# Input norms ahead of the segments, one column-tiled stretch per attention unit, feature-map adds on VectorE

## The chip, the core and the metric

One core of a Trainium2 chip runs the kernel. The metric is the device time of one execution in microseconds (us). TensorE is called PE in the rows, its weight loads PEld; DVE is VectorE, ACT is ScalarE, POOL is GpSimd, SP is SyncE, whose queue issues every DMA.

## What is computed

The input x has 2048 tokens of 1024 values (bf16). Cut to what matters, the reference is:

```python
n = layernorm(x)
q, k, v = n @ wq, n @ wk, n @ wv          # 32 heads of 32
M, z = 0, 0
for s in range(4):                        # segments of 512 tokens
    p = softmax(qs @ ks.T * scale + causal_mask)
    a_dot = p @ vs
    a_mem = (phi(qs) @ M) / (phi(qs) @ z + 1e-6)
    o = g * a_mem + (1 - g) * a_dot       # g = sigmoid(beta), per head
    M, z = M + phi(ks).T @ vs, z + phi(ks).sum()
h = x + concat(o) @ wo
out = h + (silu(m @ w1) * (m @ w3)) @ w2  # m = layernorm(h), inner width 3584
```

phi(t) is t + 1 where t > 0 and exp(t) elsewhere.

## The kernel before, in words

**Order.** The program first records all operations in a graph (`Graph`, L58), with what each reads, writes and costs, and a class: lower classes go first. `Graph.schedule` (L181) then plays the graph forward with those costs and fixes one order for each engine; `Graph.emit` (L311) writes it out with semaphore waits. So on the chip each engine runs its list in order, and an instruction that waits holds up all behind it on its engine. This is so for SP too: a load whose buffer isn't free yet holds up the loads behind it.

**Stages.** `run` (L934) records: constants, the norm and the projections of segment 0, then for each segment s: the norm of segment s+1 (`ln1`, L640), its projections (`qkv`, L653), the memory update (`memory`, L689), the attention (`attention`, L733) and the output projection with residual and second norm (`wo_stage`, L855). After that come two blocks of the feed-forward part of 1024 tokens each (`ffn_up` L878, `ffn_down` L910).

**Input norm.** `ln1` loads four tiles of 128 tokens into `xs`, of which there are two buffers (L460). `ln` (L622) takes statistics on DVE (L628, L630), the power -0.5 on POOL (L634, L636) and normalises on DVE (L637). PE transposes (L549), ACT or DVE copies the result (L560, L561) into `xnT`, of which there is one (L461): it is free again only when the projections of the segment before are done.

**Projections.** Weights come in six loads of 1 MB into three buffers `wp`; PE makes groups of eight matmuls of 512 columns (L537). Groups of full-size matmuls share two PSUM banks, 6 and 7 (`dense_group`, L523).

**Attention.** A unit (L743) is four heads of a segment; there are 32. It makes scores in three batches in PSUM banks 0 to 3 with four 32-row matmuls side by side (L763), exponentials on ACT (L778: eA, eB, eC), causal masks on POOL (L783), and then the sums with v and with ones in banks 4 and 5, four 32-column matmuls side by side (L814). These last are eight separate operations of PE, which the plan places one by one:

```python
for gr, what in ((gn, "n"), (gd, "d")):
    for kc, src in pieces():
        ...
        o = G.op("pe", 60 + (512 - 128 * kc) / 2.4, emit, reads=reads, cls=1, group=gr)
        o.mode = "col"
```

DVE inverts the sums (L824 to L844); from segment 1 on, the memory part is multiplied and added on POOL (L850, L852).

**Feature map.** `phi` (L677) makes exp on ACT, a min and a max on DVE (L682, L684) and their sum on POOL (L686), for keys (`pk`) and queries (`pq`), 24 times.

Of the kernel before, what the change touches and what calls it, by code (L numbers as in the profile page):

```python
# [10 lines left out]
BF16 = DT.bfloat16  # L11
# [5 lines left out]
class Op:  # L17
# [4 lines left out]
                 "mode", "bytes", "kind", "snap", "gate")  # L22

    def __init__(self, engs, cost, emit, cls, seq):
        self.engs, self.cost, self.emit, self.cls, self.seq = engs, cost, emit, cls, seq
        self.eng = None
        self.deps, self.users = {}, []
        self.missing = 0
        self.ready = 0.0
        self.start = self.end = None  # L30
        self.pos = None
        self.signal = False
        self.tok = None
        self.group = None
# [5 lines left out]
        self.gate = None  # L40

# [15 lines left out]

class Graph:  # L58
# [5 lines left out]
    SWITCH = 60.0  # L64
# [25 lines left out]
    def region(self, ap):  # L90
        where = self.base.get(ap.tensor.name)
# [3 lines left out]
        size = SIZE[ap.dtype]  # L95
        if space == "sb":
# [4 lines left out]
            dims = list(ap.ap)  # L101
            np_ = dims[0][1]
            ext = sum((n - 1) * abs(s) for s, n in dims[1:])
            return space, p0, p0 + np_, off + f0 * size, off + (f0 + ext + 1) * size
        ext = sum((n - 1) * abs(s) for s, n in ap.ap)
        return space, 0, 1, ap.offset * size, (ap.offset + ext + 1) * size

    def _touch(self, op, ap, write):
# [3 lines left out]
        space, p0, p1, lo, hi = reg  # L112
        step = self.PAGE if space == "sb" else 1 << 18
        for page in range(lo // step, (hi - 1) // step + 1):
            recs = self.pages.setdefault((space, page), [])
            keep = []
            for r in recs:
                o, w, a, b, c, d = r
                over = a < p1 and p0 < b and c < hi and lo < d
                if over and o is not op and (write or w):  # L120
                    self.dep(op, o, raw=w and not write)
                    if write and p0 <= a and b <= p1 and lo <= max(c, page * step) \
                            and min(d, (page + 1) * step) <= hi:
                        continue
                keep.append(r)
            keep.append((op, write, p0, p1, lo, hi))
            self.pages[(space, page)] = keep
# [7 lines left out]
    def op(self, engs, cost, emit, reads=(), writes=(), cls=5, deps=(), group=None,  # L135
           opens=False, closes=False, kind=None, gate=None):
# [6 lines left out]
        o.gate = gate  # L143
        if gate is not None:
# [7 lines left out]
        if group is not None:  # L152
            o.group = group
# [27 lines left out]
    def schedule(self):  # L181
# [15 lines left out]
        def offer(o):  # L197
            for e in o.engs:
                heapq.heappush(avail[e], (o.cls, o.seq, o))

        for o in ops:
            if o.missing == 0:
                offer(o)
        now = 0.0
        started = set()

        def can_start(o):
            g = o.group
            if g is None or g.banks is not None:
                return True  # L210
# [16 lines left out]
        while n_done < len(ops):  # L227
            moved = True
            while moved:
                moved = False  # L230
                for e in ENGINES:
# [4 lines left out]
                    while avail[e]:  # L236
                        item = heapq.heappop(avail[e])
                        o = item[2]
                        if o in started:
                            continue  # L240
                        if not can_start(o):
# [19 lines left out]
                    o.end = now + cost  # L261
# [21 lines left out]
            if what == "free":  # L283
                free[x] = True
            elif what == "pe":
# [5 lines left out]
            else:  # L291
# [8 lines left out]
                if g is not None:  # L300
# [96 lines left out]
def pool_ns(n):  # L397
    return 220.0 + n * 1.05
# [6 lines left out]
class Kernel:  # L405
# [13 lines left out]
    def plan(self):  # L419
# [40 lines left out]
        self.xs = [buf(f"xs{i}", [128, 1024], BF16) for i in range(2)]  # L460
        self.xnT = buf("xnT", [128, 8, 512], BF16)  # L461
# [30 lines left out]
        for i, off in enumerate((r1 + 16384, r2 + 4096)):  # L492
# [73 lines left out]
    def pool_op(self, f, n, reads, writes, cls=4):  # L566
        return self.g.op("pool", pool_ns(n), lambda e, gr: [f(e)], reads=reads, writes=writes,
                         cls=cls)
# [52 lines left out]

    def ln(self, k, src, dst, cls):  # L622
# [3 lines left out]
        for c in range(2):  # L626
            a, b = self.lnst[:, k, 6 * c:6 * c + 6], src[:, c * 512:(c + 1) * 512]
            self.dve_op(lambda e, a=a, b=b: e.bn_stats(a, b), dve_ns(512), [b], [a], cls)  # L628
        st2 = self.lnst[:, k, :].rearrange("p (a b) -> p a b", a=2)
        self.dve_op(lambda e: e.bn_aggr(mv, st2), 200.0, [st2], [mv], cls)  # L630
# [5 lines left out]
        self.pool_op(lambda e: e.tensor_tensor(rs, ve, mh, op=ALU.pow), 300, [ve, mh], [rs], 0)  # L636
        self.dve_op(lambda e: e.tensor_scalar(dst, src, mean, rs, op0=ALU.subtract,  # L637
                                              op1=ALU.mult), 540.0, [src, mean, rs], [dst], cls)

    def ln1(self, s):  # L640
        for i in range(4):
            t = 4 * s + i
            x = self.xs[t % 2][:, :]
            self.g.dma(x, self.x2d[t * 128:(t + 1) * 128, :], cls=0 if s == 0 else 2)
            self.ln(t, x, x, 2)
            gr = self.dense_group()
            self.transposes(gr, [(c * 128, self.xs[t % 2][:, c * 128:(c + 1) * 128])
                                 for c in range(8)], 2)
            out = self.xnT[:, :, i * 128:(i + 1) * 128]
# [3 lines left out]
    def qkv(self, s):  # L653
        p = s % 2
        for half in range(2):
            for kind in "qkv":
# [3 lines left out]
                self.g.dma(w[:, :, :], self.w[kind][:, half * 512:(half + 1) * 512].rearrange(  # L660
                    "(c p) n -> p c n", p=128), cls=1)
                for i in range(4):
                    gr = self.dense_group()
                    if kind == "v":
                        items = [(lambda gr: self.bank(gr), self.xnT[:, c, i * 128:(i + 1) * 128],
# [3 lines left out]
                    else:  # L669
                        items = [(lambda gr: self.bank(gr), w[:, c, i * 128:(i + 1) * 128],  # L670
                                  self.xnT[:, c, :], c == 0, c == 7, 512) for c in range(8)]
# [3 lines left out]
                    self.evac(gr, out, 512, view, cls=3)  # L675

    def phi(self, src, dst, cls):  # L677
# [5 lines left out]
                    [e_], [e_], cls)  # L683
        self.dve_op(lambda e: e.tensor_scalar(r, src, 0.0, None, op0=ALU.max), dve_ns(1024, 4),  # L684
                    [src], [r], cls)
        self.pool_op(lambda e: e.tensor_tensor(dst, e_, r, op=ALU.add), 1024, [e_, r], [dst],  # L686
                     cls)

    def memory(self, s):  # L689
# [3 lines left out]
        for pr in range(4):  # L693
# [29 lines left out]
            self.pool_op(lambda e, Mb=Mb, am=am, bl=bl: e.tensor_tensor(Mb, am, bl, op=ALU.mult),  # L723
                         256, [am, self.blk[:, :]], [Mb], 4)
# [18 lines left out]
    def unit(self, s, g, q, k, v, pq):  # L743
# [61 lines left out]
        for gr, what in ((gn, "n"), (gd, "d")):  # L805
            for kc, src in pieces():
                def emit(e, gr, kc=kc, src=src, what=what):
                    ins = []
                    b = gr.banks[0]
# [8 lines left out]
                    return ins  # L818

                reads = [src, v[:, kc, g, 0:128] if what == "n" else self.ones32[:, :]]  # L820
                o = G.op("pe", 60 + (512 - 128 * kc) / 2.4, emit, reads=reads, cls=1, group=gr)
                o.mode = "col"
# [4 lines left out]
        if s:  # L827
            td = t1v[:, :, 1:2]
            self.dve_op(lambda e: e.tensor_scalar(td, td, 1e-6, None, op0=ALU.add), 160.0,
                        [td], [td], 0)  # L830
# [16 lines left out]
        if s:  # L847
            spread(R1, 1)
            Nm = self.Nm[:, :]
            self.pool_op(lambda e: e.tensor_tensor(o2, Nm, R1, op=ALU.mult), 512, [Nm, R1],  # L850
                         [o2], 2)
            self.pool_op(lambda e: e.tensor_tensor(oT, o1, o2, op=ALU.add), 512, [o1, o2],  # L852
                         [oT], 2)

    def wo_stage(self, s):  # L855
        oT = self.oT[s % 2]
        for i in range(4):
# [3 lines left out]
            for half in range(2):  # L861
                gr = self.dense_group()
                self.mms(gr, [(lambda gr: self.bank(gr), oT[:, c, i * 128:(i + 1) * 128],
                               self.wo[:, c, half * 512:(half + 1) * 512], c == 0, c == 7, 512)
                              for c in range(8)], 5)
# [7 lines left out]
            gr = self.dense_group()  # L873
# [4 lines left out]
    def ffn_up(self, blk):  # L878
        for ch in range(14):
            n = self.n_w13  # L880
            self.n_w13 += 1
# [129 lines left out]
```

## Time and profile before

| | us |
|---|---|
| median of 3 runs (1021.6 to 1023.35) | 1021.63 |
| the profiled execution, its own time | 1023.85 |
| its span, first to last instruction | 1022.1 |
| PE matmul busy | 947.3 (93%) |
| DVE busy | 418.9 (41%) |
| ACT busy | 320.6 (31%) |
| POOL busy | 235.2 (23%) |
| read from HBM / written | 76.55 MB / 8.39 MB |

The rows are of one execution. Matmuls overlap each other, so a busy PE isn't PE at its peak; the granted clock says at what share of its full speed PE was let run. A busy share over the whole span mixes stages that have different limits, so the stretches are read one by one.

### The profile page before, as it was taken

The numbers are of one execution on the slowest core, as the hardware profiler recorded it, in microseconds if no ns is written. First come the engines' busy times: TensorE is split into PE (matmuls) and PEld (weight loads), VectorE is DVE, ScalarE is ACT, GpSimd is POOL, SyncE is SP. The second block draws the span as 40 slices with busy tenths as digits, with TensorE's granted clock in tenths as the row PEclk, the third lists the DMA queues.
The fourth block names the chain that finished last, engine by engine and source line by source line (L and its number), as shares of the span: only waits on it lengthen the run. The fifth ranks groups of instructions, "written<-read, shape, count | busy, mean of one in ns | idle before, by whom it ended". The sixth has DMA issues, their size and how long they took to land.

```text
span 1022.1 us, 13535 instructions
## 1 busy us (share of the span) xinstructions
PE 947.3 (93%) x5639; PEld 419.5 (41%) x5744; DVE 418.9 (41%) x710; ACT 320.6 (31%) x353; POOL 235.2 (23%) x317
## 2 busy tenths in 40 slices
PE   0899899689968999999999999999999999999998
PEld 0334344234433333344444444444444444444443
DVE  2355662766457474546343343111133333332111
ACT  1367454777266766512111111000011111110000
POOL 2244333787178765400000000000000000000000
PEclk9999899899997999999999999999999999999999
DMA  7223233212330230486222332111123222210110
GB/s 257 77 71 132 94 103 124 73 52 84 124 105 1 83 104 22 114 294 186 73 58 78 83 83 83 33 30 42 42 83 88 83 63 83 62 57 26 42 42 26
DMA packets 101965, 85.82 MB, mean 84 GB/s; under 512 B 3088, under 2 KB 89104, under 8 KB 101904
## 3 DMA queue, kind: packets, MB, share of 16 engines
q1 hardware_dynamic: 101904, 84.95, 26.9%
q8 instruction: 45, 0.74, 0.3%
q14 instruction: 16, 0.13, 0.0%
HBM read 76.55 MB, written 8.39 MB: 83 GB/s over the span
## 4 chain that ended last, share of the span: by engine, by line
PE 78%; POOL 7%; DVE 7%; ACT 2%; DMA 2%; issue 2%; SPq 1%; DVEq 0%; ACTq 0%; POOLq 0%
PE ps L537 72%; PE ps L814 3%; POOL pk L686 2%; POOL pq L686 2%; PE ps L763 2%; DMA xs<-in_A_x_dram 1%; SPq L176 1%; PE ps L549 1%; DVE h L868 1%; POOL oT L852 1%; POOL eC L783 1%; DVE phe L682 1%; POOL o L850 1%; DVE phr L684 1%; ACT phe L512 1%
## 5 line engine op out<-in xcount | busy, mean ns | idle before, releaser
L537 PE MATMUL ps<-hnT,w1b 128*128 128x512 bf16 x879 | 221.9, 379 | 2.4 <-DMA w1b<-in_B_w_dram 1.4
L537 PE MATMUL ps<-hnT,w3b 128*128 128x512 bf16 x875 | 221.2, 379 | 1.1
L898 ACT ACTIVATE sg<-ps 128x512 bf16<-128x512 f32 x112 | 66.9, 597 | 420.7 <-PE ps L537 420.7
L537 PE MATMUL ps<-w2b,hm 128*128 128x512 bf16 x877 | 195.2, 379 | 1.0
L901 DVE SCALAR_TENSOR_TENSOR t<-sg,ps 128x512 bf16<-128x512 bf16 x112 | 76.9, 687 | 224.2 <-ACT sg L898 224.2
L537 PEld LDWEIGHTS ps<-w2b,hm 128*128 128x128 bf16 x896 | 87.7, 98 | 105.7
L537 PEld LDWEIGHTS ps<-hnT,w1b 128*128 128x128 bf16 x896 | 87.2, 98 | 106.1 <-issue 5.1
L537 PEld LDWEIGHTS ps<-hnT,w3b 128*128 128x128 bf16 x896 | 87.1, 98 | 104.9 <-issue 0.9
L537 PE MATMUL ps<-xnT,wp 128*128 128x512 bf16 x492 | 122.3, 390 | 6.1 <-ACT xnT L560 3.4
L906 DVE SCALAR_TENSOR_TENSOR hm<-t,ps 128x512 bf16<-128x512 bf16 x112 | 76.8, 686 | 34.9 <-PE ps L537 31.8
L928 DVE TENSOR_TENSOR ob<-hr,ps 128x512 bf16<-128x512 bf16 x32 | 22.0, 687 | 143.4 <-PE ps L537 143.4
L537 PEld LDWEIGHTS ps<-xnT,wp 128*128 128x128 bf16 x512 | 46.7, 100 | 63.1 <-issue 15.4
L537 PE MATMUL ps<-wp,xnT 128*128 128x512 bf16 x244 | 61.3, 380 | 2.7 <-DVE v L561 1.4
L778 ACT ACTIVATE eA<-ps 128x2048 bf16<-128x2048 f32 x32 | 60.0, 1874 | 10.7 <-PE ps L763 9.0
L537 PE MATMUL ps<-wo,oT 128*128 128x512 bf16 x248 | 59.8, 379 | 1.2 <-DVE h L868 0.5
L778 ACT ACTIVATE eB<-ps 128x1536 bf16<-128x1536 f32 x32 | 46.4, 1449 | 18.0 <-PE ps L763 18.0
L778 ACT ACTIVATE eC<-ps 128x1536 bf16<-128x1536 f32 x32 | 46.3, 1448 | 17.1 <-PE ps L763 16.2
L783 POOL TENSOR_SCALAR_AFFINE_SELECT eC<-eC 128x512 bf16<-128x512 bf16 x64 | 41.9, 655 | 21.6 <-ACT eC L778 20.5
L549 PE MATMUL ps<-ident,xs 128*128 128x128 bf16 x128 | 13.2, 265 | 28.3 <-DVE xs L637 26.0
L763 PE MATMUL ps<-qT,kT 32*128 32x256 bf16 (+3 forms) x512 | 36.1, 315 | 2.8 <-ACT eC L778 1.4
L824 DVE STREAM_TRANSPOSE T<-ps 128x512 f32<-128x512 f32 x32 | 22.8, 712 | 31.9 <-PE ps L814 31.9
L537 PEld LDWEIGHTS ps<-wo,oT 128*128 128x128 bf16 x256 | 23.4, 98 | 29.5 <-issue 3.8
(88 smaller groups left out, 765.9 us busy)
## 6 DMA issues: line engine op xcount, KB each, us to landing
w1b<-in_B_w_dram SPq DMA_DIRECT2D x28, 512.0 KB, 3.9
w3b<-in_B_w_dram SPq DMA_DIRECT2D x28, 512.0 KB, 4.7
wp<-in_A_wq_dram SPq DMA_DIRECT2D x8, 1024.0 KB, 4.9
wp<-in_A_wk_dram SPq DMA_DIRECT2D x8, 1024.0 KB, 4.9
wp<-in_A_wv_dram SPq DMA_DIRECT2D x8, 1024.0 KB, 5.1
w2b<-in_B_w_dram SPq DMA_DIRECT2D x7, 1024.0 KB, 8.8
xs<-in_A_x_dram SPq DMA_DIRECT2D x16, 256.0 KB, 2.8
xr<-in_A_x_dram SPq DMA_DIRECT2D x16, 256.0 KB, 2.9
```

Of the source, the lines that this page charges most:

```text
L537: return [e.matmul(p[0](gr), p[1], p[2], start=p[3], stop=p[4]) for p in part]
L549: return [e.transpose(b[:, c:c + 128], s, self.ident[:, :]) for c, s in items]
L686: self.pool_op(lambda e: e.tensor_tensor(dst, e_, r, op=ALU.add), 1024, [e_, r], [dst], cls)
L763: ins.append(e.matmul(self.bank(gr, j, n, off), k[r, g, 128 * kc:128 * kc + 128], q[r, g, 128 * kc:512], start=True, stop=True, tile_posit ...
L778: return [e.activation(et[:, :, :], src, AF.Exp, scale=self.scale)]
L783: self.pool_op(lambda e, m=m: e.affine_select(m, m, pattern=[[0, 4], [1, 128]], compare_op=ALU.is_ge, fill=0.0, base=0, channel_multiplier ...
L814: ins.append(e.matmul(self.ps[r, b * 512 + 128 * kc:(b + 1) * 512], lhsT, src[:, j, :], start=first, stop=True, tile_position=(0, 32 * j), ...
L824: G.op("dve", dve_ns(512), lambda e, gr: [e.transpose(T1, self.bank(gr))], writes=[T1], cls=0, group=gd)
L898: self.g.op("act", act_ns(512), lambda e, gr, sg=sg: [e.activation(sg, self.bank(gr), AF.Tanh, scale=0.5)], writes=[sg], cls=2, group=gg)
L901: e.scalar_tensor_tensor(t1, sg, 1.0, self.bank(gr), op0=ALU.add, op1=ALU.mult)], reads=[sg], writes=[t1], cls=2,
L906: e.scalar_tensor_tensor(dst, t1, 0.5, self.bank(gr), op0=ALU.mult, op1=ALU.mult)], reads=[t1], writes=[dst], cls=2,
L928: self.g.op("dve", dve_ns(512), lambda e, gr, hs=hs, ob=ob: [e.tensor_tensor(ob, hs, self.bank(gr), op=ALU.add)], reads=[hs], writes=[ob], ...
```

## The change

1. `ln1` of segments 1 to 3 is recorded ahead of the segments. Their transposed results go to buffers that are otherwise used later: segments 1 and 2 to those of the first two hidden norms (`hnT`), segment 3 to the one that segment 0 has left. `xs` has four buffers in place of two. While segment 0 is normed, banks 4 and 5 serve beside 6 and 7.
2. One tile of the first segment takes its statistics on ACT. The first 1 MB of weights comes in two loads of 256 columns. Sixteen matmuls on zeros run on PE at the start.
3. The eight column-tiled operations of a unit become one, which claims banks 4 and 5 together and reads all three exponentials. The planner lets it wait up to 2.6 us for a moment at which PE is not among full-size matmuls.
4. The sum in `phi` is on DVE; its max is on DVE or ACT. The product with the block mask and the multiply and add of the memory part are on POOL or DVE, whichever is free first in the plan.
5. The output projections of segments 2 and 3 are recorded among the first feed-forward block, after chunks 3 and 7 of 14, in a later class.
6. Costs that the planner uses are other numbers (among them the change of PE's tiling, 105 in place of 60 ns, and POOL's), it counts a port that DVE and POOL share, copies out of the projections have class 1 in place of 3, and overlaps of strided regions are found exactly.

The diff, cut to its core:

```diff
-    SWITCH = 60.0
+    SWITCH = 105.0
...
-def pool_ns(n):
-    return 220.0 + n * 1.05
+def pool_ns(n, inputs=1):
+    return 170.0 + n * (0.88 if inputs == 1 else 2.1)
...
-        self.xs = [buf(f"xs{i}", [128, 1024], BF16) for i in range(2)]
-        self.xnT = buf("xnT", [128, 8, 512], BF16)
+        self.xs = [buf(f"xs{i}", [128, 1024], BF16) for i in range(4)]
+        xn = buf("xnT", [128, 8, 512], BF16)
+        self.xnT = [xn, hnT01[0], hnT01[1], xn]
...
+                        if o.patience and mode == "full" and now < o.offered + o.patience:
+                            skipped.append(item)
...
+        w = self.oT[1][:, 0, :]
+        self.dve_op(lambda e: e.memset(w, 0.0), 300.0, [], [w], 0)
+        gr = self.dense_group()
+        wl = self.oT[1][:, 0, 0:128]
+        self.mms(gr, [(lambda gr: self.bank(gr), wl, w, True, True, 512)] * 16, 0, split=16)
...
+    def either(self, f, n, inputs, reads, writes, cls, mode=1, first="pool"):
+        engs = ("pool", "dve") if first == "pool" else ("dve", "pool")
+        return self.g.op(engs, {"pool": pool_ns(n, inputs), "dve": dve_ns(n, mode)},
+                         lambda e, gr: [f(e)], reads=reads, writes=writes, cls=cls, port=True)
...
+    def ln_act(self, k, src, dst):
+        sm, nm, sq = (self.lnst[:, k, i:i + 1] for i in range(3))
+        junk = self.oT[0][:, 0:2, :].rearrange("p a b -> p (a b)")
+        G = self.g
+        G.op("act", act_ns(1024), lambda e, gr: [e.activation(junk, src, AF.Copy, accum_out=sm)],
+             reads=[src], writes=[junk, sm], cls=1)
+        self.act(nm, sm, AF.Copy, 190.0, cls=1, scale=-1.0 / 1024)
+        G.op("act", act_ns(1024, 1), lambda e, gr: [e.activation(
+            junk, src, AF.Square, bias=nm, accum_out=sq)], reads=[src, nm], writes=[junk, sq],
+            cls=1)
...
     def ln1(self, s):
...
-            x = self.xs[t % 2][:, :]
+            x = self.xs[t % 4][:, :]
...
-            self.ln(t, x, x, 2)
-            gr = self.dense_group()
+            if t == 1:
+                self.ln_act(t, x, x)
+            else:
+                self.ln(t, x, x, 2 if s == 0 else 5)
+            gr = self.dense_group() if s else Group([(6,), (7,), (4,), (5,)], safe=True)
...
-            out = self.xnT[:, :, i * 128:(i + 1) * 128]
+            out = self.xnT[s][:, :, i * 128:(i + 1) * 128]
...
+                if n == 0:
+                    self.g.dma(w[:, :, 0:256], src[:, :, 0:256], cls=1)
+                    self.g.dma(w[:, :, 256:512], src[:, :, 256:512], cls=1)
+                else:
+                    self.g.dma(w[:, :, :], src, cls=1)
...
-        self.pool_op(lambda e: e.tensor_tensor(dst, e_, r, op=ALU.add), 1024, [e_, r], [dst],
-                     cls)
+        self.dve_op(lambda e: e.tensor_tensor(dst, e_, r, op=ALU.add), dve_ns(1024, 2),
+                    [e_, r], [dst], cls, port=True)
...
+        both = Both(gn, gd)
+
+        def emit(e, gr):
+            ins = []
             for kc, src in pieces():
-                def emit(e, gr, kc=kc, src=src, what=what):
-                    ins = []
-                    b = gr.banks[0]
+                for g_, what in ((gn, "n"), (gd, "d")):
+                    b = g_.banks[0]
...
-                o = G.op("pe", 60 + (512 - 128 * kc) / 2.4, emit, reads=reads, cls=1, group=gr)
-                o.mode = "col"
+        reads = [src for _, src in pieces()] + [v[:, :, g, 0:128], self.ones32[:, :]]
+        o = G.op("pe", 2 * 1280 / 2.4, emit, reads=reads, cls=1, group=both)
+        o.mode = "col"
+        o.patience = 2600.0
...
-            self.pool_op(lambda e: e.tensor_tensor(o2, Nm, R1, op=ALU.mult), 512, [Nm, R1],
-                         [o2], 2)
-            self.pool_op(lambda e: e.tensor_tensor(oT, o1, o2, op=ALU.add), 512, [o1, o2],
-                         [oT], 2)
+            self.either(lambda e: e.tensor_tensor(o2, Nm, R1, op=ALU.mult), 512, 2, [Nm, R1],
+                        [o2], 2)
+            self.either(lambda e: e.tensor_tensor(oT, o1, o2, op=ALU.add), 512, 2, [o1, o2],
+                        [oT], 2)
...
+        for s in range(1, 4):
+            self.ln1(s)
         for s in range(4):
             if s < 3:
-                self.ln1(s + 1)
                 self.qkv(s + 1)
                 self.memory(s)
             self.attention(s)
-            self.wo_stage(s)
-        for blk in range(2):
-            self.ffn_up(blk)
-            self.ffn_down(blk)
+            if s < 2:
+                self.wo_stage(s)
+        for ch in range(14):
+            self.ffn_up(0, ch)
+            if ch == 3:
+                self.wo_stage(2)
+            elif ch == 7:
+                self.wo_stage(3)
+        self.ffn_down(0)
+        for ch in range(14):
+            self.ffn_up(1, ch)
+        self.ffn_down(1)
```

## Rows read from the trace of the kernel before

**Rows 1.** Busy time by stretch: us; PE, PEld, DVE, ACT, POOL busy (count), PEclk, DMA, GB/s.

```profile
0.00:31.00 31.00, 4.12 (x32) 3.09 (x32) 9.14 (x28) 6.20 (x9) 6.76 (x25) 1.00 0.67 221
31.00:437.00 406.00, 363.84 (x2942) 151.83 (x2993) 227.12 (x411) 246.02 (x232) 224.08 (x283) 0.96 0.27 87
437.00:1022.10 585.10, 579.30 (x2667) 264.62 (x2719) 182.62 (x274) 68.35 (x112) 4.38 (x9) 1.00 0.25 75
```

**Rows 2.** Timeline, 0 to 50 us: start, us, engine, line, operation, tiles, count, idle before.

```profile
0.79 0.86 SPq L176 DMA_DIRECT2D xs<-in_A_x_dram  x2
...
3.48 1.88 DVE L628 BATCH_NORM_STATS2 lnst<-xs 128x6 f32<-128x512 bf16 x3 [3.48 <-DMA xs<-in_A_x_dram]
...
7.25 1.04 PE L549 MATMUL ps<-ident,xs 128*128 128x128 bf16 x8 [7.25 <-DVE xs L637]
...
8.32 1.02 ACT L560 ACTIVATE xnT<-ps 128x1024 bf16<-128x1024 bf16 x1 [6.25 <-PE ps L549]
...
11.17 19.04 SPq L176 DMA_DIRECT2D xs<-in_A_x_dram  x4
...
22.91 1.88 DVE L628 BATCH_NORM_STATS2 lnst<-xs 128x6 f32<-128x512 bf16 x3 [4.59 <-DMA xs<-in_A_x_dram]
...
31.07 13.24 PE L537 MATMUL ps<-xnT,wp 128*128 128x512 bf16 x47 [1.27 <-ACT xnT L560]
```

**Rows 3.** Busy time by stretch, the first projections on PE.

```profile
31.00:36.60 5.60, 5.53 (x14) 1.93 (x15) 3.20 (x8) 0.22 (x1) 1.55 (x4) 1.00 0.13 43
36.60:44.00 7.40, 7.35 (x35) 3.32 (x34) 0.00 (x0) 2.77 (x5) 0.00 (x0) 1.00 0.24 77
```

**Rows 4.** Timeline of PE: changes of tiling; the first and the last tiled stretch.

```profile
44.24 0.40 PE L763 MATMUL ps<-qT,kT 32*128 32x512 bf16 x4
...
48.84 1.04 PE L537 MATMUL ps<-wp,xnT 128*128 128x512 bf16 x4
49.81 0.34 PE L763 MATMUL ps<-qT,kT 32*128 32x256 bf16 x8
50.08 1.04 PE L537 MATMUL ps<-wp,xnT 128*128 128x512 bf16 x4
...
436.04 0.24 PE L814 MATMUL ps<-eC,v 128*32 128x128 bf16 x4
```

**Rows 5.** Busy time by stretch: the seams between segments, and a stretch without one.

```profile
100.00:112.50 12.50, 8.49 (x112) 3.92 (x108) 9.34 (x20) 10.19 (x8) 8.60 (x18) 0.73 0.31 110
175.00:187.50 12.50, 9.58 (x97) 4.78 (x97) 5.58 (x15) 7.38 (x9) 7.40 (x5) 1.00 0.40 132
187.50:200.00 12.50, 7.49 (x103) 3.57 (x105) 11.37 (x18) 9.36 (x9) 11.99 (x15) 0.88 0.10 32
200.00:212.50 12.50, 9.20 (x98) 3.41 (x91) 12.19 (x23) 10.01 (x9) 11.20 (x17) 0.71 0.14 42
287.50:300.00 12.50, 9.02 (x116) 4.84 (x117) 7.92 (x19) 9.20 (x10) 8.34 (x8) 1.00 0.40 128
300.00:312.50 12.50, 7.22 (x86) 2.87 (x83) 10.14 (x18) 8.64 (x8) 10.82 (x13) 0.75 0.01 2
312.50:325.00 12.50, 8.82 (x79) 3.60 (x82) 8.05 (x12) 7.97 (x8) 11.77 (x16) 0.70 0.01 1
325.00:412.00 87.00, 84.64 (x695) 31.96 (x706) 48.49 (x91) 62.73 (x60) 55.62 (x65) 1.00 0.19 61
```

**Rows 6.** Instructions of the feature map (min/median/max ns), and the group of a DVE copy.

```profile
L686 POOL TENSOR_TENSOR pq<-phe,phr x12: 2112/2120/2133, 179.0 to 388.9; 128x1024 bf16<-128x1024 bf16 x12
L684 DVE TENSOR_SCALAR phr<-qT x12: 418/428/1490, 177.4 to 387.2; 128x1024 bf16<-128x1024 bf16 x12
...
L561 DVE COPY pkn<-ps 128x1024 bf16<-128x1024 bf16 x8 | 5.5, 685 | 3.0 <-PE ps L549 2.9
```

**Rows 7.** Waits of PE: engine, line, waited for, us in total, times, longest us.

```profile
PE ps L814 <- POOL eC L783: 10.0, 7, 3.3
```

**Rows 8.** DMA issues of a feed-forward weight: count, KB each, median us to landing.

```profile
w1b<-in_B_w_dram SPq DMA_DIRECT2D x28, 512.0 KB, 3.9
```

More of the change, by code (lines that the diff above doesn't have):

```diff
@@ L21 @@
                  "ready", "start", "end", "pos", "signal", "tok", "group", "first", "last",
-                 "mode", "bytes", "kind", "snap", "gate")
+                 "mode", "bytes", "kind", "snap", "gate", "port", "patience", "offered")
     def __init__(self, engs, cost, emit, cls, seq):
@@ L40, in __init__ @@
         self.gate = None
+        self.port = False
+        self.patience = 0.0
+        self.offered = 0.0
 class Group:
@@ L95, in region @@
         size = SIZE[ap.dtype]
+        dims = list(ap.ap)
         if space == "sb":
@@ L100, in region @@
             p0, f0 = divmod(ap.offset, row)
[L101 to L106, printed above, removed]
+            p1 = p0 + dims[0][1]
+            dims = dims[1:]
+        else:
+            p0, p1, f0 = 0, 1, ap.offset
+        run, outer = 1, []
+        for step, n in reversed(dims):
+            if n == 1 or step == 0:
+                continue
+            if step <= run or not outer and run == 1:
+                run += (n - 1) * step
+            else:
+                outer.append((step, n))
+        starts = [f0]
+        for step, n in outer:
+            starts = [a + step * i for a in starts for i in range(n)]
+        if len(starts) > 64:
+            starts, run = [min(starts)], max(starts) - min(starts) + run
+        return space, p0, p1, [(off + a * size, off + (a + run) * size) for a in starts]
     def _touch(self, op, ap, write):
@@ L143, in op @@
         o.gate = gate
+        o.port = port
         if gate is not None:
@@ L203, in schedule, with claim @@
                 offer(o)
-        now = 0.0
+        until = {e: 0.0 for e in ENGINES}
+        held = {"dve": 0.0, "pool": 0.0}
         started = set()
+        nudged = set()
         def can_start(o):
             g = o.group
+            if isinstance(g, Both):
+                todo = [x for x in g.parts if x.banks is None]
+                for x in todo:
+                    if x.after is not None and x.after.banks is None:
+                        return False
+                    if any(self.bank_owner[b] is not None for b in x.choices[0]):
+                        return False
+                return all([claim(o, x) for x in todo])
+            return claim(o, g)
+        def claim(o, g):
             if g is None or g.banks is not None:
@@ L260, in schedule @@
                         mode = o.mode
-                    o.end = now + cost
+                    begin = now
+                    if e == "pool":
+                        begin = max(begin, held["dve"])
+                    elif e == "dve" and o.port:
+                        begin = max(begin, until["pool"])
+                    o.end = begin + cost
+                    until[e] = o.end
+                    if e == "dve" and o.port:
+                        held["dve"] = o.end
                     lat = self.LAT.get(e, 100.0)
@@ L284, in schedule @@
                 free[x] = True
+            elif what == "look":
+                pass
             elif what == "pe":
@@ L674, in qkv @@
                     self.mms(gr, items, 6)
[L675 removed]
+                    self.evac(gr, out, 512, view, cls=1)
     def phi(self, src, dst, cls):
```

174 lines of the change are left out of this document (98 added, 76 removed).

## The prediction

> **What bounds the kernel now.** I read the busy times by stretch first. From 437 us on, PE is busy 579.3 of 585.1 us, with 2719 weight loads, one for each full-size matmul, so 0.215 us a matmul [rows 1]. That stretch is the feed-forward part at PE's own pace, and the change touches it only by moving two output projections among it, which takes and gives the same matmuls. What can be won lies ahead of 437 us, and there in three places.
>
> The first is the start: in the first 31 us PE is busy 4.12 [rows 1]. The timeline shows why. The first two token tiles are asked for at 0.79 us and the first statistics run at 3.48; the next two tiles are asked for only from 11.17 on, behind the weight loads and the reuse of two buffers, and their statistics run at 22.91; the first projection starts at 31.07 [rows 2].
>
> The second is the seams, where one segment's attention is left alone on PE because the next segment's projections still wait for their norm: seven stretches of 12.5 us with PE busy 59.8 of 87.5, five of them at a granted clock of 0.70 to 0.88 [rows 5]. A stretch of 87 us in which projections fill the gaps is busy 84.64 and granted 1.00 [rows 5].
>
> The third is changes of tiling. Four full matmuls begin at 48.84 and the next, score matmuls begin at 49.81: 0.97 us where 4 x 0.215 = 0.86 is work. Eight score matmuls, two sets of four side by side with 256 and 128 columns, take until 50.08: 0.27 where 384/512 x 0.215 = 0.16 is work [rows 4]. So one change costs about 0.10 us. In the timeline of PE I count 96 stretches of score matmuls, 139 of column-tiled ones and 160 of full ones, the first tiled one at 44.24, the last at 436.04 [rows 4]: 394 changes, 39 us.
>
> **The change, part by part.**
>
> **Start.** All four tiles are now asked for ahead of the weights. The first lands for 3.48 [rows 2]. Three more of 256 KB at 221 GB/s, the mean of the first 31 us [rows 1], take 1.2 us each: the last lands at 7.1. From landing to transposes took 7.25 - 3.48 = 3.8 us for the first tile, then 1.04 and 1.02 for transposes and copy [rows 2]: the last tile is ready at 13.0. The four tiles overlap, one of them on ACT, which does nothing between its table load and 8.32 [rows 2], so I take 12.0 for the first projection; bounds 10.5 (faster transfers) and 17 (statistics one after the other). The first half of the first weights, 512 KB, took 3.9 us to land in the feed-forward part [rows 8]: behind the tiles it is there by 11. Saved: 31.07 - 12.0 = **19.0 us**. The twelve tiles of later segments come earlier in SP's queue, behind the four and beside the weights. Each waits for its buffer there and holds the loads behind it, as now at 11.17 [rows 2]; but the wait is for a transpose near at hand, no longer for the end of a projection. I cost it at nothing; if that cover goes, a late 1 MB weight load costs some 5 us once.
>
> **Clock at the start.** The first 14 projections took 5.53 us, 0.395 each, the next 35 took 7.35, 0.21 each [rows 3]. This is half pace, as at the lower of the two levels, 1.2 and 2.4 GHz, although the granted clock of the stretch reads 1.00. Sixteen matmuls on zeros run before PE has other work, so they cost nothing; at worst they hold the first transposes, due at 7.25 [rows 2], by a microsecond. Between them and the projections PE has pauses. Gain between 0 and 14 x (0.395 - 0.215) = 2.5; I take the middle, **1.3 us**.
>
> **One column-tiled stretch a unit.** The most that can be left is 96 + 32 tiled stretches with full ones between, 256 changes; if every column-tiled stretch stands right behind scores, 224. I take 230: 164 fewer at 0.10, **16.4 us** (bounds 14 and 17). What it adds is a wait: nothing of the sums starts before the last mask (POOL, eC), and PE stands with all that is queued behind, the scores of the next unit too, if the plan had that mask earlier than the chip. PE waited for that mask 7 times, 10.0 us in all [rows 7], and this stays; more of it is in the term below.
>
> **Seams.** In the seven stretches PE idles 27.7 us; at the idle share of the filled stretch, 2.7%, it would be 2.4, so 25.3 is excess. The busy time of the five with a lowered clock, 8.49, 7.49, 9.20, 7.22 and 8.82, times what the clock lacks, 0.27, 0.12, 0.29, 0.25 and 0.30, is 10.3. Together 35.6 us [rows 5]. With the norms done early the next projections can follow as soon as weights are there, and six loads of 1 MB stay two ahead. The twelve tiles' transposes and copies aren't saved but fall in the first 100 us, among projections. The borrowed buffers push something back: the hidden norm of segment 0 may write only when segment 1 is projected, so that output projection becomes filler of the next segment. What is late next is DVE, so I don't take all: **33 us** (bounds 15 and 36).
>
> **Adds on DVE.** POOL's sum took 2.12 us, 24 times [rows 6]. On DVE no row shows it. The bounds are 0.43 (a one-input DVE instruction of the same shape, median) and POOL's 2.12; nearest is a DVE copy of as many 16-bit values out of PSUM, 0.69 [rows 6]. 24 x 0.69 = 16.6 us, and perhaps as much again where the memory part goes to DVE, in place of 227 of 406 us [rows 1]. By a stretch that is shorter by 33 + 16, DVE would be some 70% busy. It lies beside PE's work, except where DVE empties one of the two banks that full matmuls share. For that and for later sums I add **4 us**; the bounds are -5 (POOL's chain gets shorter by 24 x 1.4) and 25.
>
> A max that DVE does in 0.43 us took up to 1.49 beside POOL's sum [rows 6]: the two engines do hold each other. The Trainium skill, "GPSIMD Engine Reference", section Key points, says that POOL contends with DVE instructions of two SBUF inputs as well as with those of a 2-port mode. By that rule the sum on DVE is held by POOL's masks and holds them; it is a rival below.
>
> **Output projections later.** PE's work is the same, and feed-forward work fills attention in their place; nothing either way. The first feed-forward chunks need the projections to be over, as now.
>
> **Sum.** 19.0 + 1.3 + 16.4 + 33 - 4 = 65.7. The profiled execution took 1023.85 us with a span of 1022.1, so 1.75 lie around it; it becomes 958.2. It was 2.2 above the median of the runs, 1021.63, which becomes **956**. A measurement of this kernel can tell about 0.2% from no change.
>
> **Rivals.**
>
> *Seams stay in part* (0.16). For it: in 187.5 to 212.5 DVE is busy 23.6 of 25 us, POOL 23.2 [rows 5], so the attention itself may be slower than what fills it, and the next q, k and v can't be written while their buffers are read. Against: part of this is the norm and POOL's sums, which leave. Half the gain is 973, none of it 989.
>
> *The adds crowd DVE* (0.08). Each of 24 sums is held as the slowest max was, 1.49 - 0.43 = 1.06 us, with PE waiting: 956 + 25 = 981. For it: row 6's maximum; against: those maxima stood beside the very sums of 2.12 us that leave POOL.
>
> *The start doesn't move* (0.05): weights in 512-byte pieces or the statistics are late, and the change doesn't do what it says there: 956 + 19 = 975.
>
> *The single stretch waits* (0.04), which makes it slower. Place: PE at L814's successor, behind POOL's eC mask. If each of 32 units waits as the longest wait now, 3.3 us [rows 7], it costs 106 us: 1062. It decides from 65.7/32 = 2.1 us a unit on. Against: the sums are low in the list of what the planner takes first, and there are fillers.
>
> *PE is fed throughout* (0.08): the scattered waits shrink too, by a plan whose costs are nearer the chip, and nothing is paid for DVE: 938 or less.
>
> **How the numbers follow.** The forecast has 0.59. The range 935 to 985 takes in its bounds, the start that doesn't move, the crowded DVE and half the seams; outside are the slow rival, seams that stay whole, and the lower end of the last. Faster: all but the slow rival and a small rest, 0.93; within 0.2%, 0.02; slower, 0.05.
>
> **What would show it.** First projection near 12 us; some 230 changes of tiling in place of 394, with 32 column-tiled stretches; no stretch of 12.5 us before the feed-forward part with PE under 10 us busy and a clock under 0.9; the sum of `phi` on DVE at 0.6 to 0.9 us. Wrong would be: projections of a segment that still start after a pause of PE, waits of PE for eC above 60 us, or DVE busy above 90% over 100 us.

## The result and the profile after

The changed kernel takes 946.33 us (median of 4 runs, 944.8 to 948.32) where the kernel before takes 1021.71 beside it: a ratio of 0.926, 95% interval 0.9237 to 0.9283. The prediction was 956 with a range of 935 to 985. The gain of 75.4 us is 10 more than the 65.7 forecast, and the experiments below show that early norms, to which the prediction put down its largest term, are only one of the ways in which the change ends the seams.

The profiled execution took 944.8 us, its span is 943.1. Busy time by stretch of the changed kernel, with the columns of [rows 1]: the first two answer to the first two rows there, the third is the worst between segments of the stretches of 12.5 us counted from 0, the fourth answers to [rows 3].

```profile
0.00:31.00 31.00, 25.05 (x140) 11.28 (x143) 12.40 (x35) 16.65 (x24) 8.87 (x29) 1.00 0.91 296
31.00:437.00 406.00, 390.33 (x3219) 181.47 (x3268) 270.87 (x488) 250.49 (x248) 160.85 (x238) 1.00 0.35 109
225.00:237.50 12.50, 10.00 (x95) 4.41 (x98) 10.67 (x21) 7.85 (x7) 5.62 (x8) 1.00 0.29 84
13.00:16.20 3.20, 3.06 (x14) 1.50 (x16) 0.00 (x0) 0.33 (x1) 0.00 (x0) 1.00 1.10 352
```

PE is busy 25.05 of the first 31 us in place of 4.12 (5.13 of it the matmuls on zeros), and 390 of the next 406 in place of 364, at a granted clock of 1.00 in place of 0.96. Those 406 us now hold some 75 of the feed-forward part, since the last tiled matmul starts at 361.5 and no longer at 436.04 [rows 4]. No seam goes below 10.00 of 12.5.

The timeline of the changed kernel at the start and at the first seam (start, us, engine, line, operation, tiles, count, idle before) answers to [rows 2] and shows one column-tiled stretch:

```profile
0.79 1.81 SPq L203 DMA_DIRECT2D xs<-in_A_x_dram  x4
1.24 5.13 PE L597 MATMUL ps<-oT 128*128 128x512 bf16 x16 [1.24 <-DVE oT L651]
8.79 1.60 PE L609 MATMUL ps<-ident,xs 128*128 128x128 bf16 x24 [2.42 <-DVE xs L727]
11.27 0.61 PE L609 MATMUL ps<-ident,xs 128*128 128x128 bf16 x8 [0.88 <-DVE xs L727]
13.08 4.12 PE L597 MATMUL ps<-xnT,wp 128*128 128x512 bf16 x17 [1.21 <-ACT xnT L620]
...
80.30 0.40 PE L921 MATMUL ps<-eA,v 128*32 128x512 bf16 x4
80.53 0.39 PE L921 MATMUL ps<-eA,ones 128*32 128x512 bf16 x4
...
81.29 0.23 PE L921 MATMUL ps<-eC,v 128*32 128x128 bf16 x4
81.34 0.23 PE L921 MATMUL ps<-eC,ones 128*32 128x128 bf16 x4
81.73 0.81 PE L597 MATMUL ps<-hnT,wp 128*128 128x512 bf16 x3 [0.16 <-issue]
```

The first projection starts at 13.08 where it started at 31.07. The eight sets of column-tiled matmuls of a unit run in one go: counted as in the prediction, there are 96 stretches of scores, 32 column-tiled and 108 full, so 235 changes.

The waits of PE in the changed kernel, longest total first (engine, line, waited for: us, times, longest us):

```profile
PE ps L597 <- issue: 5.4, 34, 0.2
PE ps L609 <- DVE xs L727: 3.3, 2, 2.4
PE ps L597 <- ACT xnT L620: 1.8, 2, 1.2
PE ps L597 <- DVE h L976: 1.7, 3, 0.6
```

A wait of the column-tiled stretch (L921) for POOL's eC, 10.0 us before [rows 7], doesn't occur among PE's waits.

Of the 79.0 us between the two spans, 18.0 are the earlier start, if all of it is won, and 159 x 0.10 = 16 the changes of tiling. Some 45 are left for the seams, the clock and smaller waits. Which parts of the change earn those was for the experiments.

### The profile page after: what moved, and what is told of

Its sections match the earlier page's. It is cut to its first block, busy times and chain, and to the rows that moved or that the text cites. A ratio compares the mean times of both kernels' runs of the same rounds, so it can differ in the third digit from the quotient of the medians.

```text
span 943.1 us, 13518 instructions
## 1 busy us (share of the span) xinstructions
PE 915.6 (97%) x5661; PEld 421.3 (45%) x5760; DVE 434.7 (46%) x749; ACT 321.6 (34%) x360; POOL 172.8 (18%) x274
## 4 chain that ended last, share of the span: by engine, by line
PE 94%; ACT 2%; DVE 2%; issue 1%; DMA 1%; SPq 0%; DVEq 0%; ACTq 0%
PE ps L597 86%; PE ps L921 4%; PE ps L868 3%; PE ps L609 1%; DMA xr<-in_A_x_dram 1%; DVE h L976 1%; ACT eB L883 0%; DMA xs<-in_A_x_dram 0%; ACT eA L883 0%; DVE lnst L718 0%; ACT xnT L620 0%; ACT v L620 0%; DVE v L621 0%; ACT qT L620 0%; ACT pkn L620 0%
## 5 line engine op out<-in xcount | busy, mean ns | idle before, releaser
L597 PE MATMUL ps<-xnT,wp 128*128 128x512 bf16 x244 | 58.4, 379 | 2.9 <-issue 1.6
L597 PE MATMUL ps<-hnT,wp 128*128 128x512 bf16 x246 | 59.1, 380 | 1.4 <-issue 1.3
L888 POOL TENSOR_SCALAR_AFFINE_SELECT eA<-eA 128x512 bf16<-128x512 bf16 x32 | 21.4, 670 | 89.1 <-ACT eA L883 89.1
L597 PEld LDWEIGHTS ps<-xnT,wp 128*128 128x128 bf16 x256 | 23.1, 98 | 28.5 <-issue 3.7
```

Of the source, the lines that this page charges most:

```text
L597: return [e.matmul(p[0](gr), p[1], p[2], start=p[3], stop=p[4]) for p in part]
L888: self.pool_op(lambda e, m=m: e.affine_select(m, m, pattern=[[0, 4], [1, 128]], compare_op=ALU.is_ge, fill=0.0, base=0, channel_multiplier ...
```

## The experiments

All were timed in three rounds beside the kernel before; a difference is to the changed kernel's 946.33 unless it says otherwise.

**Late norms (952.34 us, ratio 0.9314, 0.9299 to 0.933).**

```diff
-        self.xnT = [xn, hnT01[0], hnT01[1], xn]
+        self.xnT = [xn, xn, xn, xn]
...
-        for s in range(1, 4):
-            self.ln1(s)
         for s in range(4):
             if s < 3:
+                self.ln1(s + 1)
```

The classes of `ln` and its transposes go back to 2 as well.

> The changed kernel with the norms of segments 1 to 3 back inside the segments and one buffer for their transposed results; all else of the change stays. Theory (the seams were the late norm, and early norms are worth what the seams showed): about 36 us more than the changed kernel's 946, some 982, and stretches between segments with PE under 10 of 12.5 us busy come back. Rival (the seams were POOL's sums of the feature map, which stay on DVE here): at most 10 us more, 946 to 956, with PE busy at the seams.

It costs 6.0 us, not 36. One stretch between segments with PE under 10 us busy comes back, and only one (busy time by stretch, this kernel):

```profile
75.00:87.50 12.50, 9.64 (x131) 4.62 (x120) 9.47 (x20) 7.93 (x6) 7.98 (x16) 0.86 0.28 96
```

So the late norm by itself doesn't make the seams in this kernel, and the theory fails here. The rival's reason fails too: POOL's sums, put back alone or together with late norms, make no seams either, as two runs below show.

**Eight pieces (966.1 us, ratio 0.9453, 0.9437 to 0.9469).** The block of the eight operations from the kernel before takes the place of `both` and its one operation.

```diff
-        both = Both(gn, gd)
...
-        o.patience = 2600.0
+        for gr, what in ((gn, "n"), (gd, "d")):
+            for kc, src in pieces():
...
+                o = G.op("pe", 60 + (512 - 128 * kc) / 2.4, emit, reads=reads, cls=1, group=gr)
```

> The changed kernel with the eight column-tiled operations of a unit placed one by one again, and no patience. The order has 412 changes of tiling in place of 235. Theory (a change costs 0.097 us and PE has no time to spare): 177 x 0.097 = 17 us more, 963. Rival (the single stretch waits for the last mask and so gives back what it saves): no more than 5 us more, or faster. Second rival (the pieces also wait for masks on their own, 10 us in the kernel before): some 27 us more, 973.

19.8 us more for 177 changes, 0.11 us each: the count at its price of 0.10, and some 2 us that may be waits. Waiting for masks has hardly a part in it (0.5 us in all); the longest waits of PE there are others:

```profile
PE ps L597 <- issue: 4.7, 29, 0.2
PE ps L597 <- DVE h L973: 3.9, 3, 1.5
```

**The sum on POOL (946.26 us, ratio 0.9259, 0.9242 to 0.9276).**

```diff
-        self.dve_op(lambda e: e.tensor_tensor(dst, e_, r, op=ALU.add), dve_ns(1024, 2),
-                    [e_, r], [dst], cls, port=True)
+        self.pool_op(lambda e: e.tensor_tensor(dst, e_, r, op=ALU.add), 1024, [e_, r], [dst],
+                     cls, inputs=2)
```

> The changed kernel with the sum of the feature map back on POOL, its max on DVE or ACT as in the change. Theory (the sum lies beside PE's work on either engine): within 4 us of the changed kernel, 942 to 950. Rival 1 (POOL's sums of 2.12 us are in the chain that ended the seams): 15 us or more longer, 961 up, PE waiting for pk or pq. Rival 2 (the sums crowd DVE, as the prediction charged 4 us for): 4 us or more faster, 942 or less.

No difference. The instructions of the feature map (min/median/max ns), first in the changed kernel, then in this one:

```profile
L791 DVE TENSOR_TENSOR pk<-phe,phr x12: 627/693/1714, 34.7 to 218.8; 128x1024 bf16<-128x1024 bf16 x12
L791 DVE TENSOR_TENSOR pq<-phe,phr x12: 675/689/1382, 145.8 to 326.1; 128x1024 bf16<-128x1024 bf16 x12
```

```profile
L791 POOL TENSOR_TENSOR pk<-phe,phr x12: 2115/2118/2126, 28.0 to 221.6; 128x1024 bf16<-128x1024 bf16 x12
L791 POOL TENSOR_TENSOR pq<-phe,phr x12: 2121/2124/2565, 148.3 to 331.5; 128x1024 bf16<-128x1024 bf16 x12
```

The sum takes 0.69 on DVE and 2.12 on POOL. Among PE's waits in either kernel there is none for `pk` or `pq`, and the time is the same.

**Old start (956.19 us, ratio 0.9355, 0.9337 to 0.9373).**

```diff
-            x = self.xs[t % 4][:, :]
+            x = self.xs[t % 2][:, :]
...
-            if t == 1:
-                self.ln_act(t, x, x)
-            else:
-                self.ln(t, x, x, 2 if s == 0 else 5)
-            gr = self.dense_group() if s else Group([(6,), (7,), (4,), (5,)], safe=True)
+            self.ln(t, x, x, 2 if s == 0 else 5)
+            gr = self.dense_group()
...
-                if n == 0:
+                if n < 0:
```

> The changed kernel with the first loads as before: two buffers for token tiles, the first weights in one load, all statistics on DVE, banks 6 and 7 alone; the 16 matmuls on zeros and the early norms stay. Theory (PE is short of time from its first projection to the end, so a late start is paid in full): the first projection at about 31 us and 18 us more, 964. Rival (attention's chain has slack that takes up a later start): 5 us more or less, about 951.

9.9 us, between the two. The timeline of PE in this kernel says why in the main:

```profile
15.57 5.56 PE L597 MATMUL ps<-wp,xnT 128*128 128x512 bf16 x16 [6.62 <-DMA wp<-in_A_wv_dram]
26.06 0.78 PE L609 MATMUL ps<-ident,xs 128*128 128x128 bf16 x8 [4.93 <-DVE xs L727]
27.14 1.01 PE L609 MATMUL ps<-ident,xs 128*128 128x128 bf16 x8 [0.30 <-DVE xs L727]
28.38 2.36 PE L597 MATMUL ps<-wp,xnT 128*128 128x512 bf16 x7 [0.22 <-issue]
```

Sixteen projections for v run at 15.57, for the two tiles that are there, while the other two are still to come. In the kernel before no projection stood ahead of the fourth tile. Steady work starts at 28.38, 15.3 us later than in the changed kernel, of which 3.4 (16 x 0.215) is done already. That leaves 11.9; where the other 2 us are made up, no run shows. What lets the v projections go ahead is the last part of item 6 of the change: overlaps of strided regions are found exactly. Planned with overlaps as before, this kernel has no projection ahead of the fourth tile (a plan that was built, not run). Before, the copy of a tile into `xnT`, a strided region, counted as all that lies between its first and last byte, and so as nearly all of the buffer.

**Early norms alone, in the kernel before (998.47 us, ratio 0.9764, 0.975 to 0.9779).** The first diff the other way round, in the old kernel.

> The kernel before with one part of the change: the norms of segments 1 to 3 recorded ahead, with the borrowed buffers (two token buffers as before). The order has 427 changes of tiling, 27 more than before, which costs 2.6 us. Theory as predicted (the late norm made the seams, 35.6 us): 1022 - 36 + 3, some 989. Rival (early norms are one of several ways out, and alone in the old plan they aren't enough, since attention itself crawls at the seams): 1005 or more.

23.8 us less than the 1022.25 beside it; with the 2.7 that 27 more changes of tiling cost, early norms are worth 26.5. The theory's 36 is an overestimate, but early norms alone do most of it. What stays are seams of a milder kind, at a granted clock of 1.00 (busy time by stretch, this kernel):

```profile
162.50:175.00 12.50, 9.26 (x89) 4.65 (x87) 5.39 (x12) 8.25 (x9) 7.04 (x4) 1.00 0.38 125
262.50:275.00 12.50, 9.70 (x100) 4.92 (x99) 5.86 (x14) 7.38 (x9) 7.55 (x5) 1.00 0.34 111
```

So norms are worth 24 us alone and 6 in company: another part of the change must end the seams too. Three runs look for it among token buffers, planner costs and POOL's sum.

**Late norms, two token buffers (949.77 us, ratio 0.9287, 0.927 to 0.93).** Late norms as above, and

```diff
-            x = self.xs[t % 4][:, :]
+            x = self.xs[t % (2 if s else 4)][:, :]
```

> The changed kernel with late norms and one transposed buffer, and besides, from segment 1 on, only two token buffers in place of four. Theory (with four buffers a whole segment can be normalised ahead and only transposes and copies are late, which is why late norms alone cost 6 us): the seams come back, 25 us above the changed kernel or more, 971 up. Rival (token buffers don't matter; the plan with truer costs, or POOL's freed time, closes the seams): as late norms alone, 950 to 956.

The token buffers are not it.

**Old planner costs (948.58 us, ratio 0.9273, 0.926 to 0.9287).**

```diff
-    SWITCH = 105.0
+    SWITCH = 60.0
...
-    return 170.0 + n * (0.88 if inputs == 1 else 2.1)
+    return 220.0 + n * 1.05
...
-        o.port = port
+        o.port = False
```

The other costs and classes that the expectation names go back in the same way.

> The changed kernel with the planner's old numbers: change of tiling 60 ns, POOL's old cost, no shared port, old costs and classes of statistics, copies of projections in class 3. Theory (the order changes a little, PE stays fed): within 6 us of the changed kernel, 941 to 952. Rival (the truer costs are what closes gaps): 15 us more or above, 961 up.

2.3 us, with the intervals of the two ratios overlapping: costs and classes hardly matter beside the rest. But the norms are early in this kernel; whether truer costs would stand in for early norms, it can't tell, and late norms with nothing else but old costs weren't run.

**Late norms and the sum on POOL (953.84 us, ratio 0.9328, 0.9312 to 0.9344).** Both diffs together.

> The changed kernel with late norms, one transposed buffer, and the sum of the feature map on POOL. Theory (the two don't help each other): as late norms alone, 948 to 957. Rival (either of the two is enough to close the seams, which is why undoing one costs little): 20 us more than the changed kernel or above, 966 up.

The two don't stand in for each other either.

**The single stretch without most of the rest (980.05 us, ratio 0.9591, 0.9569 to 0.9612).** Late norms, the sum on POOL, the old start and the old planner costs as above, no matmuls on zeros and early output projections as below, all in one kernel.

> The changed kernel with late norms, old start, no matmuls on zeros, the sum of the feature map on POOL, early output projections and the planner's old numbers: of the change there stay the single column-tiled stretch, the choice of engine for the memory part and the max, and the exact overlaps. The order has 232 changes of tiling, 168 fewer than before. Theory 1 (the stretch saves the changes and no more): 1022 - 16 = 1006, with the seams as before. Theory 2 (it also ends the seams, which is why late norms cost only 6 us beside it): 985 or less.

42.2 us less than the 1022.25 beside it. Some 17 are the 168 changes of tiling. Up to 8 are won at the start, where v projections go ahead here too: by 44 us PE has made 40 matmuls more than in the kernel before, of which 4 are scores and 36 projections, and 36 x 0.215 is 7.7. Busy time by stretch, the first 44 us of the kernel before and of this one, then two stretches between segments of this one:

```profile
0.00:44.00 44.00, 17.00 (x79) 8.34 (x80) 12.34 (x34) 9.19 (x14) 8.31 (x29) 1.00 0.53 174
0.00:44.00 44.00, 26.33 (x119) 11.96 (x120) 14.21 (x37) 11.35 (x18) 8.47 (x29) 0.92 0.56 185
162.50:175.00 12.50, 9.02 (x71) 4.62 (x74) 8.60 (x15) 8.00 (x9) 7.30 (x6) 1.00 0.48 144
237.50:250.00 12.50, 8.70 (x105) 4.31 (x103) 10.85 (x19) 9.78 (x10) 8.76 (x11) 1.00 0.32 111
```

That leaves 17 or more, and the total is what theory 2 had. The seams haven't all gone, though: these two stretches are the milder kind again. And theory 2 puts the 17 down to the single stretch, which the next run speaks against.

**Late norms and eight pieces (967.0 us, ratio 0.9457, 0.9439 to 0.9476).** The first two diffs together.

> The changed kernel with late norms and with the eight column-tiled operations one by one; all else of the change stays. If the two undone parts add: 946 + 6 + 20 = 972, 968 to 976. If either of them is enough to end the seams, so that undoing one shows little: 985 or more, with stretches of 12.5 us under 10 us busy between segments.

0.9 us more than eight pieces with early norms. With neither early norms nor the single stretch the seams don't come back. What the last two kernels share, and the kernel before lacks, is what no diff had undone: exact overlaps, and the choice of engine for the memory part and the max. The cause needn't be one that they share, since the second also keeps the new costs and the sum on DVE; but these two are where to look first.

The timelines tell these two apart. First PE in the kernel before at its second seam, then PE in the kernel with the single stretch at the same seam, only rows of projections (`wp`) and of the norm's transposes (`xs`):

```profile
181.58 1.03 PE L537 MATMUL ps<-wp,xnT 128*128 128x512 bf16 x4
183.84 0.62 PE L549 MATMUL ps<-ident,xs 128*128 128x128 bf16 x8
187.31 0.62 PE L549 MATMUL ps<-ident,xs 128*128 128x128 bf16 x8
198.12 1.03 PE L549 MATMUL ps<-ident,xs 128*128 128x128 bf16 x8 [0.55 <-DVE xs L637]
207.37 0.62 PE L549 MATMUL ps<-ident,xs 128*128 128x128 bf16 x8
210.00 1.02 PE L537 MATMUL ps<-xnT,wp 128*128 128x512 bf16 x4 [0.61 <-ACT xnT L560]
```

```profile
163.84 0.62 PE L609 MATMUL ps<-ident,xs 128*128 128x128 bf16 x8 [0.47 <-DVE v L621]
164.75 1.90 PE L597 MATMUL ps<-wp,xnT 128*128 128x512 bf16 x8 [0.30 <-ACT pkn L620]
167.64 0.62 PE L609 MATMUL ps<-ident,xs 128*128 128x128 bf16 x8 [0.44 <-DVE v L621]
168.57 1.90 PE L597 MATMUL ps<-wp,xnT 128*128 128x512 bf16 x8 [0.31 <-ACT pkn L620]
170.76 1.89 PE L597 MATMUL ps<-wp,xnT 128*128 128x512 bf16 x8
174.40 0.62 PE L609 MATMUL ps<-ident,xs 128*128 128x128 bf16 x8 [1.76 <-DVE xs L722]
178.07 0.62 PE L609 MATMUL ps<-ident,xs 128*128 128x128 bf16 x8 [0.62 <-DVE Macc L814]
179.85 1.46 PE L597 MATMUL ps<-xnT,wp 128*128 128x512 bf16 x6 [0.66 <-issue]
```

In the kernel before, no tile of the next segment is transposed until the last projection is out, and 27 us pass between the end of the last and the start of the next projection. With exact overlaps and the same single `xnT`, the first two tiles go in among the last v projections, as soon as each tile's part of the buffer has been read, and 7 us pass. Every list shows it; these are the full-size projection matmuls (192 a segment) that the list of PE has ahead of each of the 16 tiles. The second kernel is the one before with exact overlaps alone, the fourth is late norms and eight pieces without them; these two were built but not run on the chip.

```
before                              0 0  0  0  192 192 192 192  384 384 384 384  576 576 576 576
before + exact overlaps             0 0 16 16  168 176 192 192  360 368 380 384  552 560 572 576
late norms, eight pieces            0 0  0  0  176 176 188 192  360 368 376 384  560 560 576 576
the same, overlaps as before        0 0  0  0  192 192 192 192  384 384 384 384  576 576 576 576
early norms in the kernel before    0 0  0  0   24  28  52  56   72  84 100 104  192 192 216 220
changed kernel                      0 0  0  0   96 100 104 104  144 144 144 144  184 192 192 192
```

The choice of engine can't let a transpose pass a projection; exact overlaps do. That they are what moves the transposes is shown by the lists. What they are worth by themselves in us wasn't run, nor the choice of engine alone; so how the 17 us split stays open. The planner's own total is no measurement (it misses the measured spans by up to 21 us), but it too says that the overlaps aren't the only way out: exact overlaps take 21 us off it in the kernel before, and only 4 in late norms and eight pieces.

**No matmuls on zeros (945.57 us, ratio 0.9251, 0.9235 to 0.9267).**

```diff
-        self.mms(gr, [(lambda gr: self.bank(gr), wl, w, True, True, 512)] * 16, 0, split=16)
```

> The changed kernel without the 16 matmuls on zeros. Theory as predicted: 0 to 2.5 us more, with the first projections at half pace (0.43 us each) for some microseconds. Rival (the transposes ahead of the projections are enough to keep PE at full pace): no difference, the first projections 0.22 us apart.

No difference. The timeline of PE in this kernel:

```profile
9.25 2.74 PE L609 MATMUL ps<-ident,xs 128*128 128x128 bf16 x24 [9.25 <-DVE xs L722]
12.47 0.61 PE L609 MATMUL ps<-ident,xs 128*128 128x128 bf16 x8 [0.48 <-DVE xs L722]
14.28 6.06 PE L597 MATMUL ps<-xnT,wp 128*128 128x512 bf16 x27 [1.21 <-ACT xnT L620]
```

With the zeros the first 24 transposes are faster (1.60 us in the changed kernel, 2.74 here) and the first projection is 1.2 us earlier, but the projections run at full pace from the first one here too, 27 in 6.06 us. The 1.2 us don't show in the total.

**Early output projections (946.49 us, ratio 0.9261, 0.9242 to 0.928).**

```diff
-            if s < 2:
-                self.wo_stage(s)
+            self.wo_stage(s)
...
-                gr = self.dense_group(s >= 2)
+                gr = self.dense_group()
```

> The changed kernel with the output projections of segments 2 and 3 recorded after their attention again, in class 5 and on banks 6 and 7. Theory as predicted (PE has the same work and fillers enough): within 2 us of the changed kernel, 944 to 949. Rival (in the last attention they hold the banks from feed-forward work and let PE wait for their chain of residual, norm and transposes): 4 us more or above.

No difference, as predicted.

## Why the prediction was right, point by point

**Start.** 19.0 forecast, 18.0 seen (13.08 where 12.0 stood, a little short of the bound of the tile that comes last). What a late start costs in this plan is less, 9.9, in part because the plan then fills the gap with v projections. The prediction took every us of the start for a us of the whole; that isn't so here. The rival that the start doesn't move is out.

**Clock.** 1.3 forecast; the first projections now run at full pace, 14 busy in 3.06 us from 13.08 on where 14 took 5.53 [rows 3], so some 2.5. The cause given, matmuls on zeros, is wrong: without them the pace is the same.

**Single stretch.** 230 changes forecast, 235 seen; 16.4 us forecast, and putting the pieces back costs 19.8 for 177 changes, or 14.7 where the norms are late (967.0 against 952.34). The wait for the last mask that the slow rival rested on does not occur.

**Seams.** 33 of 35.6 us were put down to early norms. Here the account was right and not complete: the late norm made most of the seams of the kernel before, and early norms alone bring 23.8 us there, within the bounds of 15 and 36. But the prediction costed what the planner's new numbers and exact overlaps do at nothing (the numbers stand in a rival only), and didn't speak of the overlaps at all. They let the next segment's tiles in among the last projections. So undoing early norms costs 6.0, not 33: there is more than one way out of the same wait. What the seams themselves gave back in the changed kernel, no run measures apart from the rest. The rival that the seams stay in part is out there.

**Adds on DVE.** 4 us of loss forecast, none found (946.26 with the sum on POOL). The price was right, 0.69 us by median for 0.69 forecast, and DVE busy 236.67 of the 348 us from 12 to 360, 68%, stands near the 70%. But PE waits for none of the sums.

The prediction read one row wrongly here. The slowest maxima of the kernel before did not stand beside POOL's sums of 2.12 us, but beside the multiply and add of the memory part (and the others above 0.6 us beside these or the masks), so the argument that the cause leaves POOL does not hold. In the changed kernel the same instructions of POOL still lengthen what DVE does. Timelines of DVE and POOL, first the longest max in the kernel before, then the longest sum in the changed kernel:

```profile
313.07 1.44 POOL L852 TENSOR_TENSOR oT<-o,o 128x512 bf16<-128x512 f32 x1
313.30 1.49 DVE L684 TENSOR_SCALAR phr<-qT 128x1024 bf16<-128x1024 bf16 x1
...
181.56 1.27 POOL L958 TENSOR_TENSOR o<-Nm,R1b 128x512 f32<-128x512 f32 x1
181.66 1.71 DVE L791 TENSOR_TENSOR pk<-phe,phr 128x1024 bf16<-128x1024 bf16 x1
182.97 1.53 POOL L960 TENSOR_TENSOR oT<-o,o 128x512 bf16<-128x512 f32 x1
```

The rule of the Trainium skill, "GPSIMD Engine Reference", section Key points, that POOL contends with DVE instructions of two SBUF inputs, agrees with the trace as far as single instructions go: the longest sum took 1.71 us. No share of it shows in the time.

**Output projections later.** Nothing forecast, nothing found.

The sum came out 10 us short. 4 are what DVE was to cost, 1.2 is more of clock, and the start moved by 1.0 less; some 6 are left, which no run assigns (of the rivals, PE fed throughout was nearest, at 938). Undone one by one, the parts are worth 6.0 + 19.8 - 0.1 + 9.9 + 2.3 - 0.8 + 0.2 = 37 of the 75 us. Six of them, all but the 19.8, are undone together in the kernel with the single stretch; there they cost 33.7 (980.05 against 946.33), where their sum is 17.5. So some of them do stand in for each other. Late norms with the sum on POOL (7.5) and late norms with eight pieces (20.7) are not such pairs; which parts are, stays open. The exact overlaps and the choice of engine no run undid.

That the total came so close is in part luck: the start's 19.0 is worth 9.9 and the seams' 33 is worth 6.0 when undone, and what makes up for it in the changed kernel has no term in the sum.

## What to carry to other kernels

Where a plan is made from recorded reads and writes, look at how an overlap is judged before a buffer is added: a strided region taken as all between its ends can order two things that never touch. A wait that two parts of a change can each take away doesn't come back when one of them is undone; run each part alone as well as each part undone. And price changes of tiling by count: it was the part whose worth undone (19.8, and 14.7 beside late norms) was nearest to that on paper (16.4).

## What the runs showed of the hardware that was not expected

The granted clock read 1.00 in stretches of half pace and of full pace alike at the start of a kernel: 14 matmuls in 5.53 us [rows 3] and 14 in 3.06. The pace of single matmuls had to be read from their starts. And without matmuls on zeros, 24 transposes in a row took 2.74 us at the slower pace, and the eight transposes (0.61 us) and the projections behind them ran at full pace. The kernel before had made its 32 transposes eight at a time, with pauses between (1.12 us and more), and then ran 14 projections at half pace.
